# Attention and FFN on one core: quad 5 loaded and rearranged one step sooner, quad 8 later

## The chip, the cores and the metric

The kernel runs on one core of a Trainium2 chip. A core has five engines that run side by side, each through its own list of instructions in order: TensorE (PE in the profile, with its weight loads as PEld), VectorE (DVE), ScalarE (ACT), GpSimd (POOL) and SyncE (SP). They wait for one another by semaphores. Transfers are issued by POOL, SP and ACT and carried out by 16 DMA engines, which all of them share. The metric is the device time of one launch in microseconds (us), and less is better. Before the change the median of 11 runs is 386.49 us (386.11 to 389.3).

## The reference

Attention without a softmax (relu squared instead), then a feed-forward layer with a leaky activation whose slope is learnt:

```python
def _attn_ref(q, k, v):                     # 8 batches, 12 heads, 448 tokens, 64 wide
    scores = scale * np.matmul(q, k.transpose(0, 1, 3, 2))
    attn = np.maximum(scores, 0.0) ** 2 / S
    return np.matmul(attn, v)

def _moe_ref(x, w_in, w_out, alpha):        # 3584 tokens, 768 wide, 2048 inside
    h = x @ w_in
    g = np.maximum(h, 0.0) + alpha * np.minimum(h, 0.0)
    return g @ w_out
```

The heads of a token, side by side, are the row `x`. All inputs and the output are float32 in memory.

## The kernel before, in words

The four heads of one batch that are worked on together are called a quad here; 8 batches make 24 quads, n = 0 to 23. All work in SBUF is in bf16.

*Loads.* POOL issues the loads of q, k and v (`load_qk`, L100; `load_v`, L107) and of the weights (`load_w_in`, L117; `load_w_out`, L122), and they turn float32 into bf16 on the way. w_out is held as two tiles: `w_out[0]` with the first 256 columns, `w_out[1]` with the other 512; a call loads 4 of 16 row groups at a time. The raw q and k have three buffers each, so quad n + 3 can only be loaded when quad n has been read. A further rule is in the program that the compiler makes of it: each load of POOL waits for the landing of the eighth before it.

*Turning.* Scores need q and k with the head's width on the partitions. The first five quads are transposed by PE (`turn_pe`, L156, copied out at L159). From quad 5 on `turn_dma` does it: two DVE copies put the rows into the order that is wanted (tile `perm`, L164, two buffers), and SP issues one transposing DMA (L166) into the tile `T` (four buffers). SP also issues nearly all output DMAs (L274), in program order with the transposes. `landed` (L376) is a copy of one element of quad 5's `T` by POOL: it does nothing but hold POOL's later loads until that transpose has landed.

*Attention.* A quad has seven chunks of keys. For a chunk, `score_mm` (L178) makes the scores in a pair of PSUM banks, `relu` takes them out on ACT (L187) or DVE (L189), and `square` (L195 on ACT, L197 on DVE) squares them. Chunks whose square is still to come stand in the list `late`; `sq(k, eng)` squares the first k of them, and each FFN1 step squares one (L252). `attnv(n)` (L207) multiplies a quad's squares by v and writes its part of xT (L217, L218).

*FFN.* `f1(b, ff)` makes one of 16 steps of FFN1 for batch b: 6 matmuls (L241), a negated relu on ACT (L249), and a combination on DVE (L250) into gT. `f2(sb, c, h)` makes 128 tokens of FFN2 for two batches, 256 or 512 columns (h = 0 or 1), with 16 matmuls (L266), a copy to SBUF on ACT (L268) and two output DMAs.

*Order.* Nothing is scheduled by a planner: the order of the calls in the source is the order on each engine. After the first three quads, FFN1 of batch 0 is mixed with the scores of quads 3 and 4, then come the first three FFN2 groups of 256 columns, the rest of quad 4, quad 5, FFN1 of batch 1 (during which quads 7 and 8 are rearranged), and FFN2 of batches 0 and 1 mixed with quads 6 to 8. From there the pattern repeats. `prepare(n)` is `turn_dma(n)` followed by the loads of quad n + 2. The score chunks from quad 6 on are taken in order by `some(k)`, so quad 8's first chunk is the 15th; `run(some(3))` after `f2(0, 3, 1)` takes it.

Of the kernel before, what the change touches and what calls it, by code (L numbers as in the profile page):

```python
# [20 lines left out]
def kernel(  # L21
# [48 lines left out]
    def take(lo, n):  # L70
        clock[0] += 1
        for i in range(lo, lo + n):
            taken[i] = clock[0]
# [12 lines left out]
    def take_bank():  # L86
        i = min(range(8), key=lambda i: (taken[i], i))
        take(i, 1)
        return psum[:, i]
# [4 lines left out]
    def load_qk(n, names="qk"):  # L94
        b, g = divmod(n, NG)
        for name in names:
            src = q if name == "q" else k
            t = raw_pool.tile([128, 2, NJ, D], BF16, tag=name, name=f"{name}raw")
            flat = src[b].rearrange("(m two) (pp j) d -> (two pp) m (j d)", two=2, j=NJ)
            nc.gpsimd.dma_start(out=t.rearrange("p m j d -> p m (j d)"), in_=flat[:, 2 * g:2 * g + 2])  # L100
            raw[(n, name)] = t

    def load_v(n):
        b, g = divmod(n, NG)
        t = v_pool.tile([128, 2, NJ, D], BF16, tag="v", name="vraw")
        flat = v[b].rearrange("(m two) (pp j) d -> (two pp) m (j d)", two=2, j=NJ)
        nc.gpsimd.dma_start(out=t.rearrange("p m j d -> p m (j d)"), in_=flat[:, 2 * g:2 * g + 2])  # L107
        vraw[n] = t
# [11 lines left out]
    def load_w_out(h, lo=0, hi=KF, step=4):  # L120
        for lo in range(lo, hi, step):
            nc.gpsimd.dma_start(out=w_out_sb[h][:, lo:lo + step], in_=w_out_v[:, lo:lo + step, COLS[h][0]:COLS[h][1]])  # L122
# [38 lines left out]
    def turn_dma(n):  # L161
        p = perm_pool.tile([128, 2, NJ, 2, D], BF16, tag="perm", name="perm")
        for i, name in enumerate("qk"):
            nc.vector.tensor_copy(p[:, i], raw.pop((n, name)).rearrange("p s j d -> p j s d"))  # L164
        t = T_pool.tile([128, 2, NJ, 128], BF16, tag="T", name="T")
        nc.sync.dma_start_transpose(out=t.rearrange("p a j c -> p (a j) c"),  # L166
                                    in_=p.rearrange("p a j s d -> p (a j s d)"))
        T[n] = t
# [23 lines left out]
    def square(n, j, rl, eng="D"):  # L192
        a = at_pool.tile([128, 2, S], BF16, tag="at", name="at")
        if eng == "A":
            nc.scalar.activation(a, rl, ACTF.Square)  # L195
        else:
            nc.vector.tensor_tensor(a, rl, rl, ALU.mult)  # L197
        att[(n, j)] = a
# [21 lines left out]
    late = []  # L220

    def sc(chunks):

        for n, j, eng in chunks:
            late.append((n, j, relu(score_mm(n, j), eng)))

    def sq(k=99, eng="D"):
        for g in late[:k]:
            square(*g, eng)
        del late[:k]  # L230

    def run(chunks):
        sc(chunks)
        sq()
# [4 lines left out]
    def f1_mm(ps, b, ff, ks):  # L239
        for km in ks:  # L240
            nc.tensor.matmul(ps, w_in_sb[:, km // 2, km % 2, bass.ts(ff, 128)],  # L241
                             xT[b][:, km // 2, km % 2, :],
                             start=(km == 0), stop=(km == KM - 1))

    def f1_out(ps, b, ff):
        if b // 2 not in gT:
            gT[b // 2] = g_pool.tile([128, KF, 2 * S], BF16, tag="g", name="gT")
        neg = neg_pool.tile([128, S], F32, tag="neg", name="neg")
        nc.scalar.activation(neg, ps, ACTF.Relu, scale=-1.0)  # L249
        nc.vector.scalar_tensor_tensor(gT[b // 2][:, ff, (b % 2) * S:(b % 2) * S + S],  # L250
                                       neg, beta_sb[:, ff:ff + 1], ps, ALU.mult, ALU.add)
        sq(1)  # L252

    def f1(b, ff):
        ps = take_bank()[:, :S]
        f1_mm(ps, b, ff, range(KM))
        f1_out(ps, b, ff)

    def f2(sb, c, h, parts=None):

        first_col, width = COLS[h][0], COLS[h][1] - COLS[h][0]
        o = o_pool.tile([128, d_model - CUT], F32, tag="o", name="osb")
        for lo, hi in parts or ((0, width),):
            ps = take_bank()[:, :hi - lo]
            for ff in range(KF):
                nc.tensor.matmul(ps, gT[sb][:, ff, bass.ts(c, 128)], w_out_sb[h][:, ff, lo:hi],  # L266
                                 start=(ff == 0), stop=(ff == KF - 1))
            nc.scalar.copy(o[:, lo:hi], ps)  # L268
            for u in range(2):
                blk = 2 * c + u  # L270
                b, j = 2 * sb + blk // NJ, blk % NJ
                rows = out[b * S:(b + 1) * S].rearrange("(pp j) d -> j pp d", j=NJ)
                eng = nc.scalar if u and parts else nc.sync
                eng.dma_start(out=rows[j][:, first_col + lo:first_col + hi], in_=o[64 * u:64 * u + 64, lo:hi])  # L274
# [4 lines left out]
    def ch(n, lo, hi, p=pat):  # L279
        return [(n, j, p[j]) for j in range(lo, hi)]  # L280
# [22 lines left out]
    sq(1)  # L303
    sc([(1, 4, "D"), (1, 5, "A"), (1, 6, "A")])
    sq(2)
    load_w_out(0, 0, 8)
    load_qk(5)
    load_v(3)
    load_w_out(0, 8)
    early = {}  # L310
# [31 lines left out]
    def f1s(b, lo, hi):  # L342
        for ff in range(lo, hi):
            f1(b, ff)

    def load(n):
        if n < NQ:
            load_qk(n)
            load_v(n)
# [13 lines left out]
    f1_mm(ps, 0, 9, range(KM))  # L363
    turn_pe(4, (("q", 0, NJ, "A"), ("k", 0, NJ, "D")))
    f1_out(ps, 0, 9)
    f1s(0, 10, 12)
    sc(ch(3, 6, 7) + ch(4, 0, 2, "AA"))
    turn_dma(5)
    f1s(0, 12, 13)
    kept = late[:]  # L370
    del late[:]
    f1s(0, 13, 16)
    late += kept
    load_qk(6)
    load_qk(7, "q")
    nc.gpsimd.tensor_copy(landed, T[5][:1, 0, 0, :1])  # L376
    load_qk(7, "k")
    load_qk(8)
    load_w_out(1)
    load_v(6)  # L380
    f2(0, 0, 0)
    sq()
# [23 lines left out]
    def some(k):  # L406
        lo = at_c[0]
        at_c[0] = min(lo + k, len(chunks))
        return [(n, j, e) for (n, j), e in zip(chunks[lo:at_c[0]], "ADA")]
# [18 lines left out]
    for ff in range(KF):  # L428
        if ff < 5:
            f1_mm(psum[:, early[ff], :S], 1, ff, range(4, KM))  # L430
            f1_out(psum[:, early[ff], :S], 1, ff)
            take(early[ff], 1)
        else:
            f1(1, ff)
        if ff in (1, 10):
            turn_dma(7 + ff // 9)
        if ff == 1:
            load(10)
    f2(0, 3, 0)
    run(some(3))  # L440
    f2(0, 0, 1)
    run(some(3))
    f2(0, 1, 1)
    f2(0, 2, 1)
# [71 lines left out]
```

## Time and profile before

| | |
|---|---|
| median of 11 runs | 386.49 us |
| profiled execution, its own time | 387.24 us |
| its span (first to last instruction) | 385.3 us |
| PE busy | 375.0 us, 97% |
| DVE, ACT, POOL busy | 266.1, 206.8, 67.8 us |
| DMA moved | 43.42 MB, mean 113 GB/s |

The page puts the span into 40 equal slices, with the busy share of each engine in tenths. A chain of work that ended last is followed back from the last instruction, from each instruction to what released it. A wait names the instruction that waited, what ended the wait, the total in us, how often and the longest. In views in order of time a row has its start and its length in us, the engine, the source line, the operation, what it writes and reads, and in brackets the engine's idle time before it and what ended that. A DMA's row is the time in which it was issued; its landing is told apart.

### The profile page before, as it was taken

The page shows a single profiled execution, that of the slowest core. Times are in us where ns is not written, and L with a number is a line of the kernel's source. Part 1 is how long each engine was busy: PE and PEld are TensorE (multiplying, and loading weights), DVE is VectorE, ACT ScalarE, POOL GpSimd, SP SyncE. Part 2 cuts the span into 40 slices and gives each one's busy share as a digit, 9 for nine tenths or more (in the row PEclk, how much of TensorE's full clock was granted, in tenths as well). Part 3 has the DMA queues.
Part 4 walks back from the last instruction along what each step waited for, and adds up shares of the span by engine and source line. Part 5 has one row for each costly group of instructions (what it writes and reads, how often), then busy time and mean ns, then how long its engine had stood idle before and what let it go on. Part 6 is the DMA issues. An engine that isn't in the chain of part 4 may idle for free.

```text
span 385.3 us, 7838 instructions
## 1 busy us (share of the span) xinstructions
PE 375.0 (97%) x3178; PEld 205.9 (53%) x3200; DVE 266.1 (69%) x422; ACT 206.8 (54%) x331; POOL 67.8 (18%) x102
## 2 busy tenths in 40 slices
PE   7799989999999999999999999999999999999996
PEld 6444554545554455555465455544556445645554
DVE  3987987765768888689655897779855788526300
ACT  4977686545364664555445555637544375434321
POOL 8557236222202202022100222020000000000000
PEclk9999999999999999999999999999999999999999
DMA  9999999999892675698292871946036300120023
GB/s 158 190 202 202 201 126 216 180 194 228 160 192 50 112 126 90 115 142 114 53 161 59 145 122 43 173 67 124 20 79 94 77 0 16 43 68 2 14 68 84
DMA packets 73284, 43.42 MB, mean 113 GB/s; under 512 B 40352, under 2 KB 69792, under 8 KB 73248
## 3 DMA queue, kind: packets, MB, share of 16 engines
q0 software_dynamic: 26864, 22.45, 39.4%
q1 hardware_dynamic: 45952, 20.07, 27.0%
q8 instruction: 25, 0.41, 0.4%
q10 hardware_dynamic: 432, 0.39, 0.3%
q14 instruction: 11, 0.09, 0.1%
HBM read 45.62 MB, written 11.01 MB: 147 GB/s over the span
## 4 chain that ended last, share of the span: by engine, by line
PE 91%; DMA 4%; DVE 3%; issue 0%; ACT 0%; ACTq 0%
PE psum L241 38%; PE psum L266 37%; PE psum L178 9%; PE psum L207 8%; DMA T<-perm 3%; DVE at L197 2%; DMA qfirst<-in_q_dram 1%; PE psum L156 1%; DVE T L159 1%; DVE rl L189 1%; ACT osb L268 0%; ACTq L274 0%; DVE qraw L140 0%
## 5 line engine op out<-in xcount | busy, mean ns | idle before, releaser
L266 PE MATMUL psum<-w_out,gT 128*128 128x256 bf16 (+3 forms) x890 | 149.8, 322 | 1.2
L241 PE MATMUL psum<-xT,w_in_sb 128*128 128x448 bf16 x768 | 149.9, 353 | 0.0
L266 PEld LDWEIGHTS <-gT 128*128 128x128 bf16 x912 | 86.7, 98 | 64.2 <-issue 8.2
L241 PEld LDWEIGHTS <-w_in_sb 128*128 128x128 bf16 x768 | 73.6, 98 | 73.0 <-issue 5.7
L250 DVE SCALAR_TENSOR_TENSOR gT<-neg,beta_sb,psum 128x448 bf16<-128x448 f32 x128 | 83.5, 677 | 35.6 <-ACT neg L249 35.5
L249 ACT ACTIVATE neg<-psum 128x448 f32<-128x448 f32 x128 | 69.2, 546 | 61.2 <-PE psum L241 59.4
L187 ACT ACTIVATE rl<-psum 128x896 bf16<-128x896 f32 x113 | 97.9, 931 | 2.6 <-PE psum L178 2.6
L197 DVE TENSOR_TENSOR at<-rl 128x896 bf16<-128x896 bf16 x164 | 91.6, 616 | 0.0
L189 DVE TENSOR_SCALAR rl<-psum 128x896 bf16<-128x896 f32 x55 | 59.7, 1086 | 40.3 <-PE psum L178 40.2
L268 ACT COPY osb<-psum 128x256 f32<-128x256 f32 (+3 forms) x57 | 26.9, 473 | 104.4 <-PE psum L266 98.7
L178 PE MATMUL psum<-T 64*64 64x448 bf16 x672 | 44.7, 356 | 3.8 <-DVE T L159 1.4
L100 POOL DMA_DIRECT2D qraw<-in_q_dram x23 | 16.6, 720 | 156.6 <-DVE perm L164 149.7
L207 PE MATMUL psum<-at,vraw 64*64 64x448 bf16 x672 | 36.6, 350 | 0.3 <-DVE at L197 0.2
L178 PEld LDWEIGHTS <-T 64*64 64x64 bf16 x672 | 16.5, 105 | 22.5 <-issue 12.5
L207 PEld LDWEIGHTS <-vraw 64*64 64x64 bf16 x672 | 20.9, 106 | 12.6 <-issue 2.3
L218 DVE TENSOR_SCALAR xT<-psum 128x448 bf16<-128x448 f32 x23 | 14.4, 624 | 14.5 <-PE psum L207 10.9
L107 POOL DMA_DIRECT2D vraw<-in_v_dram x24 | 17.5, 728 | 7.3 <-DMA w_out<-in_moe_w_out_dram 4.3
L100 POOL DMA_DIRECT2D kraw<-in_k_dram x23 | 16.6, 722 | 6.1 <-DMA w_out<-in_moe_w_out_dram 3.4
L217 ACT ACTIVATE xT<-psum 128x448 bf16<-128x448 f32 x23 | 12.6, 549 | 2.6 <-PE psum L207 2.6
L164 DVE COPY perm<-qraw 128x896 bf16<-128x896 bf16 x19 | 11.6, 611 | 0.0
L164 DVE COPY perm<-kraw 128x896 bf16<-128x896 bf16 x19 | 11.5, 608 | 0.0
L117 POOL DMA_DIRECT2D w_in_sb<-in_moe_w_in_dram x16 | 10.1, 633 | 7.4 <-DMA kraw<-in_k_dram 2.6
(25 smaller groups left out, 41.7 us busy)
## 6 DMA issues: line engine op xcount, KB each, us to landing
out_dram<-osb SPq DMA_DIRECT2D x54, 128.0 KB, 2.4
vraw<-in_v_dram POOLq DMA_DIRECT2D x24, 224.0 KB, 8.0
qraw<-in_q_dram POOLq DMA_DIRECT2D x23, 224.0 KB, 5.4
kraw<-in_k_dram POOLq DMA_DIRECT2D x23, 224.0 KB, 7.1
out_dram<-osb SPq DMA_DIRECT2D x56, 64.0 KB, 2.2
w_in_sb<-in_moe_w_in_dram POOLq DMA_DIRECT2D x16, 192.0 KB, 8.5
w_out<-in_moe_w_out_dram POOLq DMA_DIRECT2D x4, 512.0 KB, 11.6
w_out<-in_moe_w_out_dram POOLq DMA_DIRECT2D x4, 256.0 KB, 8.9
```

Of the source, the lines that this page charges most:

```text
L100: nc.gpsimd.dma_start(out=t.rearrange("p m j d -> p m (j d)"), in_=flat[:, 2 * g:2 * g + 2])
L164: nc.vector.tensor_copy(p[:, i], raw.pop((n, name)).rearrange("p s j d -> p j s d"))
L178: nc.tensor.matmul(ps[64 * c:64 * c + 64, r, :S], t[64 * r:64 * r + 64, 1, j, 64 * c:64 * c + 64], t[64 * r:64 * r + 64, 0, :, 64 * c:64 * ...
L187: nc.scalar.activation(rl, ps[:, :, :S], ACTF.Relu)
L189: nc.vector.tensor_scalar(rl, ps[:, :, :S], 0.0, None, ALU.max)
L197: nc.vector.tensor_tensor(a, rl, rl, ALU.mult)
L207: nc.tensor.matmul(ps[64 * s:64 * s + 64, r, :S], vv[64 * r:64 * r + 64, s, j, :], a[64 * r:64 * r + 64, s], start=(j == 0), stop=(j == NJ ...
L241: nc.tensor.matmul(ps, w_in_sb[:, km // 2, km % 2, bass.ts(ff, 128)], xT[b][:, km // 2, km % 2, :], start=(km == 0), stop=(km == KM - 1))
L249: nc.scalar.activation(neg, ps, ACTF.Relu, scale=-1.0)
L250: nc.vector.scalar_tensor_tensor(gT[b // 2][:, ff, (b % 2) * S:(b % 2) * S + S], neg, beta_sb[:, ff:ff + 1], ps, ALU.mult, ALU.add)
L266: nc.tensor.matmul(ps, gT[sb][:, ff, bass.ts(c, 128)], w_out_sb[h][:, ff, lo:hi], start=(ff == 0), stop=(ff == KF - 1))
L268: nc.scalar.copy(o[:, lo:hi], ps)
```

## The change

Five calls move. Rows 4 to 7 of 16 of w_out's first 256 columns are loaded after quad 5's q and k instead of before them. Quad 5 is rearranged right after FFN1's step 11 of batch 0, ahead of three score chunks and of a square that stood before it; a square of quad 3 that is left over by that goes to ACT after step 15. Both q and k of quad 7 are loaded after `landed` (before, q stood ahead of it). w_out's 512 columns are loaded ahead of quad 8's q and k. And quad 8 is rearranged, and its transpose issued, after FFN2's first group of 512 columns, instead of after step 10 of batch 1's FFN1; what is computed is the same.

```diff
     sq(2)
-    load_w_out(0, 0, 8)
+    load_w_out(0, 0, 4)
     load_qk(5)
+    load_w_out(0, 4, 8)
     load_v(3)
     load_w_out(0, 8)
@@
     f1_out(ps, 0, 9)
-    f1s(0, 10, 12)
+    f1s(0, 10, 11)
+    kept = late[:]
+    del late[:]
+    f1s(0, 11, 12)
+    turn_dma(5)
+    late += kept
     sc(ch(3, 6, 7) + ch(4, 0, 2, "AA"))
-    turn_dma(5)
     f1s(0, 12, 13)
     kept = late[:]
     del late[:]
     f1s(0, 13, 16)
     late += kept
+    sq(1, "A")
     load_qk(6)
-    load_qk(7, "q")
     nc.gpsimd.tensor_copy(landed, T[5][:1, 0, 0, :1])
-    load_qk(7, "k")
+    load_qk(7)
+    load_w_out(1)
     load_qk(8)
-    load_w_out(1)
     load_v(6)
@@
-        if ff in (1, 10):
-            turn_dma(7 + ff // 9)
         if ff == 1:
+            turn_dma(7)
             load(10)
     f2(0, 3, 0)
     run(some(3))
     f2(0, 0, 1)
+    turn_dma(8)
     run(some(3))
```

## The prediction

> **What bounds the kernel now.** I read the page first (busy shares, the 40 slices), then the chain that ended last, then the waits of TensorE (PE), then the order of time on each engine around the one wait found, and last the landing times of the single transposing DMAs. "Quad n" is a group of four heads; T5 to T9 are the transposed q and k of quads 5 to 9.
>
> ```profile
> PE 375.0 (97%) x3178; PEld 205.9 (53%) x3200; DVE 266.1 (69%) x422; ACT 206.8 (54%) x331; POOL 67.8 (18%) x102
> PE   7799989999999999999999999999999999999996
> ```
>
> PE is busy 375.0 of 385.3 us, so it sets the time; only time in which PE idles can be won, and only new PE idling can be lost. The first two and the last slice are the start and the tail, which the change doesn't touch. PE's waits between 40 and 110 us are one line:
>
> ```profile
> PE psum L178 <- DMA T<-perm: 1.0, 1, 1.0
> ```
>
> and the chain shows where:
>
> ```profile
> 41.02 2.71 PE psum L241 x14
> 43.74 10.62 DMA T<-perm
> 54.36 0.04 issue
> 54.41 0.76 PE psum L178 x12
> ```
>
> This is T5: issued at 43.74, landed 54.36, while PE had nothing left to do from 53.42 (0.99 us idle before its score matmuls at 54.41). VectorE (DVE) and GpSimd (POOL) around it, in order of time (start, duration):
>
> ```profile
> 41.38 0.67 DVE L250 SCALAR_TENSOR_TENSOR gT<-neg,beta_sb,psum 128x448 bf16<-128x448 f32 x1
> 41.97 0.62 DVE L197 TENSOR_TENSOR at<-rl 128x896 bf16<-128x896 bf16 x1
> 42.51 0.61 DVE L164 COPY perm<-qraw 128x896 bf16<-128x896 bf16 x1
> 43.04 0.61 DVE L164 COPY perm<-kraw 128x896 bf16<-128x896 bf16 x1
> ...
> 42.09 0.71 POOL L100 DMA_DIRECT2D qraw<-in_q_dram  x1 [0.41 <-issue]
> 54.42 0.18 POOL L376 COPY landed<-T 1x1 bf16<-1x1 bf16 x1 [11.61 <-DMA T<-perm]
> 54.90 0.71 POOL L100 DMA_DIRECT2D kraw<-in_k_dram  x1 [0.30 <-PE psum L178]
> ```
>
> The rearrangement starts as soon as DVE reaches it (no idle before it), and POOL is held 11.61 us at `landed`, with quad 7's q already queued ahead of it. The DMA engines are full on both sides of that stretch (columns: stretch, its length, busy time of PE, PEld, DVE, ACT, POOL, clock, DMA share, GB/s):
>
> ```profile
> 20.00:50.00 30.00, 30.00 (x303) 15.55 (x296) 25.33 (x43) 22.56 (x37) 14.52 (x21) 1.00 1.29 201
> 50.00:58.00 8.00, 7.01 (x87) 4.79 (x85) 6.70 (x11) 6.29 (x10) 3.13 (x6) 1.00 1.08 110
> 58.00:92.00 34.00, 33.90 (x229) 16.70 (x230) 22.66 (x38) 17.45 (x29) 12.88 (x18) 1.00 1.25 197
> ```
>
> Two later rows price the other half of the change, quad 8: ScalarE's (ACT's) copy of FFN2's first 512-column result, which SyncE's (SP's) output DMA waits for, and the first scores that read T8:
>
> ```profile
> 83.33 0.58 ACT L268 COPY osb<-psum 128x512 f32<-128x512 f32 x1 [2.20 <-PE psum L266]
> ...
> 99.43 0.76 PE L178 MATMUL psum<-T 64*64 64x448 bf16 x12
> ```
>
> [...] The packet records agree: with T8 in flight both queues move some 178 packets a microsecond[...]; and the outputs issued behind T8 (from 82.97) move only after it has landed at 92.94. [...] The landings agree: 5.7 us from issue for T6, which met a nearly empty POOL queue, 10.6 for T5 and 16.4 for T7, which met a full one. [...] Here T5's bar on SP is 5.33 us and its landing 10.62 after issue, so I count landings.
>
> **The change, part by part.** In the compiled order PE's instructions are unchanged in kind and order. So the change acts only on when PE's inputs land and when PSUM is freed.
>
> 1. *Rows of quad 5 ahead of rows 4 to 7 (of 16) of w_out's first 256 columns.* One 256 KB load moves behind two of 224 KB. In order of landing that load took 39.30 − 37.96 = 1.34 us, so q5 and k5 land 1.3 us sooner (40.43 to 39.1, 41.56 to 40.2). By itself worth nothing in before's order (DVE arrives at 42.51); with part 2, DVE arrives at 41.97 and k5 would have been there with 0.4 us to spare; now 1.8. The moved w_out rows land by 41.6, read from 45.9 at the earliest (FFN2 starts at 45.52): hidden, 4 us of cover.
>
> 2. *Rearrangement of quad 5 one FFN1 step sooner.* The 0.54 us square that stood ahead of it goes behind, so the two copies start at 41.97, and T5's issue goes from 43.74 to 43.2: 0.54 us gained. One square (quad 3, j = 6) goes from DVE to ACT after the 16th FFN1 step. Price 0.93 to 0.95 (ACT's squares at 50.86); ACT idles 1.20 us there, from 46.26 to its FFN2 copy at 47.46: hidden, 0.25 us of cover left; beyond it, it would delay that copy only, whose PSUM bank is not needed until later. DVE does one square less. Cost 0.
>
> 3. *Quad 7's q behind `landed`, POOL's order after it.* The load of q7 leaves the queue that T5 shares: its landing (53.37) came 1.53 us after k6's (51.84); at 201 GB/s its 224 KB is 1.1 us of the engines. So T5 has 0.54 us of head start and 1.1 to 1.5 us less traffic. Bounds on T5's landing: no better than now if something else held it (54.36), and 54.36 − 0.54 − 1.5 = 52.3 at best; I take the gains as partly overlapping, 52.8. PE needs it by 53.37 (its own 53.42 less the 0.05 from landing to matmul): a gain of 0.99 suffices. The wait goes, **0.99 us**. What is late next: T5's scores come 0.99 us sooner, at 53.42; ACT is free at 53.83, before its first relu would be due (53.85); DVE finishes rearranging quad 6 at 53.80 and its relu, at 55.10 now, would start at 54.1. Nothing is late by 0.1 us. The rearrangement of quad 6 needs k6, landed 51.84, at 52.66.
>
> 4. *w_out's 512 columns ahead of quad 8's rows.* After `landed` (sooner by 1.5) POOL issues q7, k7, four w_out loads, q8, k8. The last w_out load lands now at 75.40; with one 224 KB load less in front net and an earlier start it lands near 72; FFN2 reads it from 79.67. It wasn't waited for: 0. Quad 8's rows go from 63.36 to about 75; the rearrangement needs them at 81.3: hidden by 6 us.
>
> 5. *Rearrangement of quad 8 behind FFN2's first 512-column group.* The two copies (1.14 us on DVE) go from 72.84 to right after the squares that end at 82.30, less the 0.99 us: 81.3 to 82.45. DVE's next instruction, a relu at 83.85 now, is due at 82.86: hidden by 0.4. On SP, T8 comes behind the two outputs of that group: ACT's copy ends 83.92 − 0.99 = 82.9, two issues at some 0.58 each, T8 issued at 84.1 instead of 74.04. It must land by 99.43 − 0.99 = 98.4: **14.3 us** are there. T7 showed its first packets 3.7 us after issue (66.31 to 70.0); T8's transfer is 1,792 packets of 256 bytes, 10.1 us at 178 a microsecond: landing at 97.9 with POOL's queue full to the end. POOL's loads of quad 11 now wait for this rearrangement (from 82.5, not 80.27), those of quad 12 for quad 9's; when T8's packets begin (87.8) I count about six loads left, 6 × 1.53 = 9.2 us (the spacing of landings in that stretch), so the last of T8 moves alone: near 97. Hidden, by 0.5 to 1.5 us, where now it has 6.5 (landed 92.94). T9 follows at about 102, needed by 106.5; T7 no longer has T8 behind it and is needed at 90. The outputs behind T8 are six or so tiles of 10 in their pool: no wait.
>
> Sum: −0.99 (wait for T5) + 0 + 0 + 0 + 0. Profiled execution: 387.24 (385.3 span, 1.9 around it) to 386.25. It stands 0.75 above the median; if all of that were a longer wait for T5, the usual run would have only 0.24 of it to lose. So the gain in the median lies in 0.24 to 0.99; I take 0.9, as launch or tracing can as well make the 0.75: **385.6**.
>
> **Rivals.**
> *T5 is no earlier.* Its slowest packets at 51 to 53 us aren't q7's but its own. For it: POOL's queue has almost run out of packets by 51, and T5 still takes 3 us. Against: T6 took 5.7 us in all when alone. Then only the 0.54 counts at best: 386.0 to 386.5.
>
> *T8 becomes the wait* (the other side). Place: scores of quad 8's first chunks, 98.4. Price: each us that T8 lands after 98.4 is PE idle. At T7's measured 16.4 us from issue it lands at 100.5, 2.1 us late: 386.49 − 0.9 + 2.1 = 387.7; at T8's own 18.9 us of before, 103.0, 4.6 late: 390.2. It is slower by over 0.3% from 16.4 us on. For it: the two transposes issued in that full stretch took just these. Against: 18.9 includes waiting for T7 until 82.7; T7 shared with w_out's larger packets (148 a microsecond) and with a slice near 73 us in which all packets were slow; and the POOL queue runs dry sooner now.
>
> *More is won.* Where the usual run waits longer for T5 than the profiled one: 1.6 us gained, 384.9. Only the spread of the eleven runs (386.11 to 389.3) speaks for it.
>
> **How the numbers follow.** 0.3% (1.16 us), about what a measurement of this kernel can tell from no change, puts the bounds at 385.33 and 387.65. Wait gone and T8 in time: 0.55, own range 385.2 to 386.3, about a third of it beyond the bound, since the whole wait is 0.26%. T5 no earlier: 0.12, no change. T8 late: 0.22, most of it over 387.65. More won: 0.11. Faster 0.19 + 0.11 = 0.30; slower 0.20; the rest 0.50. The range from 384.9 leaves half the last case below, and to 387.8 most of the T8 case above.
>
> **What would show it.** Right: T5 issued near 43.2 and landed before 53.4, no wait of PE for T in 40 to 110, POOL's `landed` near 53, T8 issued near 84 and landed by 98, PE's first scores of quad 5 at 53.4, the span about 384.3. Wrong: a wait of the score matmuls (L178) for T at 53 or at 98, ACT's added square delaying the FFN2 copy past 47.5, DVE's copies waiting for q6, k6 or q8, k8.

## The result and the profile after

The changed kernel is slower. Its median is 393.11 us over 12 runs (387.69 to 398.04), against 386.23 us over 44 runs (385.61 to 389.3) of the kernel before. The ratio is 1.0106, with a 95% interval of 1.0083 to 1.0129; it leaves out runs more than 1.5% above the fastest of the same kernel, so it stands below the quotient of the medians. The scatter is new: the kernel before keeps most of its runs within 0.7 us.

The profiled execution of the changed kernel took 387.69 us, with a span of 385.9: it is the fastest of its runs. Its busy shares hardly differ from before:

```profile
PE 375.1 (97%) x3178; PEld 206.1 (53%) x3200; DVE 265.8 (69%) x421; ACT 207.8 (54%) x332; POOL 68.0 (18%) x102
PE   7799999999899999999999999999999999999996
```

There is one 8 in PE's row, in the 11th slice (96 to 106 us). The waits of PE between 40 and 110 us (total, times, longest):

```profile
PE psum L178 <- DMA T<-perm: 1.6, 1, 1.6
```

The line reads as before, with 1.6 in place of 1.0, but it is another transpose. The chain that ended last tells which (start, length):

```profile
49.81 3.60 PE psum L266 x32
53.41 0.69 PE psum L178 x12
...
82.92 1.17 PE psum L266 x5
84.09 15.95 DMA T<-perm
100.04 0.04 issue
100.08 0.76 PE psum L178 x12
```

At 53.41 quad 5's scores follow FFN2 without a gap: the wait for T5 is gone. At 100.08 quad 8's scores wait for T8, issued at 84.09 and landed at 100.04. PE was ready 1.65 us before that. The start of the change, on VectorE, GpSimd and ScalarE in order of time:

```profile
41.37 0.67 DVE L250 SCALAR_TENSOR_TENSOR gT<-neg,beta_sb,psum 128x448 bf16<-128x448 f32 x1
41.96 0.61 DVE L164 COPY perm<-qraw 128x896 bf16<-128x896 bf16 x1
42.49 0.61 DVE L164 COPY perm<-kraw 128x896 bf16<-128x896 bf16 x1
```

```profile
51.85 0.39 POOL L381 COPY landed<-T 1x1 bf16<-1x1 bf16 x1 [10.59 <-DMA T<-perm]
52.34 0.72 POOL L100 DMA_DIRECT2D qraw<-in_q_dram  x1
```

```profile
46.15 0.94 ACT L195 ACTIVATE at<-rl 128x896 bf16<-128x896 bf16 x1
47.45 0.37 ACT L268 COPY osb<-psum 128x256 f32<-128x256 f32 x1 [0.36 <-PE psum L266]
```

The square is gone from ahead of the two copies, they start at 41.96, and POOL is released at 51.85 instead of 54.42. The first load behind `landed` goes out at 52.34; before, at 54.90. SP's own rows show what that does to the next transposes (start and time of issue, not of transfer). The one of T6 before:

```profile
53.87 1.52 SPq L166 DMA_TRANSPOSE T<-perm  x1
```

And after:

```profile
53.87 7.57 SPq L166 DMA_TRANSPOSE T<-perm  x1
...
65.24 10.50 SPq L166 DMA_TRANSPOSE T<-perm  x1
...
84.09 5.42 SPq L166 DMA_TRANSPOSE T<-perm  x1
```

The first is T6, at the same 53.87 as before. It took SP 1.52 us to issue then, and takes 7.57 now. Its landing came 5.7 us after issue before, and comes 18.4 us after it now. The busy times by stretch (length, PE, PEld, DVE, ACT, POOL, clock, DMA share, GB/s):

```profile
50.00:58.00 8.00, 8.00 (x97) 5.14 (x95) 7.75 (x13) 6.40 (x11) 6.05 (x9) 1.00 0.76 112
84.00:100.00 16.00, 14.33 (x118) 7.09 (x118) 10.61 (x17) 7.24 (x11) 3.79 (x6) 1.00 1.26 202
```

PE wins back its 0.99 us in the first stretch, and loses 1.65 in the last. The span says the same: 385.3 − 0.99 + 1.65 = 385.96, measured 385.9. So one wait was traded for a larger one. But that is only the fastest run, and the median is 5 us above it.

The landings, from issue to landing in us, of the traces that matter below. "2nd" is a later trace of the changed kernel, of a run of 392.15 us; the other columns are experiments. The last row has the transfer that PE waited for, and how long.

| | before | changed | 2nd | T6 held | T8 early | T6, T8 held |
|---|---|---|---|---|---|---|
| T5 | 43.74 to 54.36 | 43.19 to 51.80 | 42.79 to 51.96 | 42.94 to 51.72 | 43.20 to 51.83 | 43.34 to 52.62 |
| T6 | 53.87 to 59.60 | 53.87 to 72.26 | 53.47 to 68.72 | 53.61 to 58.20 | 53.87 to 70.17 | 54.02 to 58.50 |
| T7 | 66.31 to 82.67 | 65.24 to 85.60 | 64.84 to 82.86 | 65.09 to 81.82 | 65.25 to 83.96 | 65.47 to 82.75 |
| T8 | 74.04 to 92.94 | 84.09 to 100.04 | 84.61 to 101.62 | 83.83 to 100.04 | 73.98 to 94.22 | 84.24 to 97.13 |
| T9 | 93.60 to 102.29 | 92.25 to 104.75 | 93.79 to 110.97 | 92.58 to 107.02 | 96.03 to 107.57 | 92.56 to 100.00 |
| PE waits | T5, 0.99 | T8, 1.65 | T8, 3.63 | T8, 1.91 | w_out, 1.08 | none |

### The profile page after: what moved, and what is told of

It is laid out like the page before. It is cut to its first block, busy times and chain, and to the rows that moved or that the text cites. A ratio compares the mean times of both kernels' runs of the same rounds, so it can differ in the third digit from the quotient of the medians.

```text
span 385.9 us, 7838 instructions
## 1 busy us (share of the span) xinstructions
PE 375.1 (97%) x3178; PEld 206.1 (53%) x3200; DVE 265.8 (69%) x421; ACT 207.8 (54%) x332; POOL 68.0 (18%) x102
## 4 chain that ended last, share of the span: by engine, by line
PE 90%; DMA 5%; DVE 3%; issue 0%; ACT 0%; ACTq 0%
PE psum L241 38%; PE psum L266 35%; PE psum L178 8%; PE psum L207 8%; DMA T<-perm 4%; DVE at L197 2%; DMA qfirst<-in_q_dram 1%; PE psum L156 1%; DVE T L159 1%; DVE rl L189 1%; ACT osb L268 0%; ACTq L274 0%; DVE qraw L140 0%
```

## The experiments

Two theories stood at first. A: T8's later issue alone makes T8 late. B: the late issue is harmless, and T8 is late because `landed` comes sooner, the loads then get ahead of T6, and the whole train of transposes is pushed back. All ratios are to runs of the kernel before on the same chip. Each diff is against the kernel that its expectation names first.

### The changed kernel again

> The changed kernel once more, for a second trace and a second set of times. If the wait for T8 (landed 100.04, 1.6 us late in the first trace) is what costs, a run at 391 us or above must show a longer wait of the score matmuls for T8, some 1.6 us plus the excess over 387.7 (5 us at 391), or further waits for T6 or T7; all other waits of PE stay as they are. If something else costs (matmuls that run slower by themselves), the wait stays near 1.6 us and the excess is spread over the span.

388.19 to 392.37 us in four runs, median 390.09, ratio 1.0103 (1.0062 to 1.0145). The trace fell on the fastest of them again (388.19, span 386.2): PE waits 1.96 us for T8, landed at 100.36, and for nothing else after 20 us. A run above 391 came into a trace only later (below). It confirms the first of the two expectations in kind, a longer wait for T8 and no other, but not in size: the wait was 3.63 us where some 6 were forecast. The rest was matmuls that ran slower (twelve score matmuls in 1.33 us in place of 0.76), which is a part of the second expectation.

### T8 issued late, and nothing else changed

```diff
-        if ff in (1, 10):
-            turn_dma(7 + ff // 9)
         if ff == 1:
+            turn_dma(7)
             load(10)
     f2(0, 3, 0)
     run(some(3))
     f2(0, 0, 1)
+    turn_dma(8)
```

> The kernel before, with only quad 8's rearrangement and transpose moved behind FFN2's first 512-column group. Theory A (the late issue alone makes T8 late, since any transpose issued into a full POOL queue takes about 16 us): T8 issued near 85.1, landed near 101, needed at 99.4, so PE waits 1.5 us or more on top of the 1.0 for T5: 387.7 us or above, with runs as scattered as the changed kernel's. Theory B (the late issue is harmless, T8 was late because T6 and T7 were pushed back by loads that begin sooner after landed): T6 lands near 60 as before, T7 near 81, T8 14 us after issue or sooner: 386.2, no change.

386.95 us in the median of 14 runs, ratio 1.0025 (1.0017 to 1.0034). In the trace T8 is issued at 83.75 and lands at 98.72, after 15.0 us; PE's scores wait 0.67 us, until 98.76. (The list of waits puts this down to a copy of ACT that ended at the same 98.72. But in the kernel before, these scores start at 99.43, ahead of that copy at 99.54, so they don't need it.) T6 lands at 60.81. So A holds in kind: the late issue does cost, with T6 landing only 1.2 us later than before. But it costs 0.25%, less than A's 387.7, and the runs stay within 386.3 to 388.0: it isn't the whole loss. This trace also shows T5 landing at 52.96 in the order of before, with no wait for it: the wait of 0.99 us isn't in every run of the kernel before.

### Quad 5 sooner, T8 as early as before

```diff
     load_qk(7)
-    load_w_out(1)
     load_qk(8)
+    load_w_out(1)
@@
-        if ff == 1:
-            turn_dma(7)
+        if ff in (1, 10):
+            turn_dma(7 + ff // 9)
+        if ff == 1:
             load(10)
@@
-    turn_dma(8)
```

> The changed kernel, with quad 8's rearrangement back after step 10 of batch 1's FFN1 and quad 8's rows ahead of w_out's 512 columns again; quad 5 sooner as in the change. Theory A: the wait for T5 stays gone and T8 is in time: 385.3 us (1.0 below before), T6 landing near 72 as in the changed kernel, T7 near 84, T8 near 95, needed at 98.4. Theory B: the transposes are still pushed back from T6 on, PE waits for T7 or T8 by 1 us or more: 387 us or above.

389.32 us in the median of 4 runs, ratio 1.0098 (1.0059 to 1.0137). T8 is in time (94.22), so A's forecast of 385.3 is wrong: the first half of the change costs about as much alone as the whole change. B's time is right, but not its wait. T6 takes 16.3 us and T7 18.7, which both theories expected, and what PE waits for in the trace isn't a transpose:

```profile
PE psum L266 <- DMA w_out<-in_moe_w_out_dram: 1.1, 1, 1.1
```

It is the last load of w_out's 512 columns, which lands at 82.41 (75.40 before, 75.46 in the changed kernel, where quad 8's rows are behind it). So with loads released early, T6 moves beside everything that comes behind `landed`, and the loads are late as well as the transposes. The traced run is the fastest of the four (span 385.4). What the two at 390 and 391 us waited for wasn't traced.

### POOL held for T6 instead of T5

```diff
-    nc.gpsimd.tensor_copy(landed, T[5][:1, 0, 0, :1])
-    load_qk(7)
-    load_w_out(1)
-    load_qk(8)
-    load_v(6)
     f2(0, 0, 0)
@@
     turn_dma(6)
+    nc.gpsimd.tensor_copy(landed, T[6][:1, 0, 0, :1])
+    load_qk(7)
+    load_w_out(1)
+    load_qk(8)
+    load_v(6)
     load_qk(9)
```

> The changed kernel, with POOL held until T6 has landed in place of T5, so that no load runs beside T6. T6 lands 6 us after issue (60) in place of 18. Theory A: T8 is still issued at 84.1 into a full queue, lands near 100, PE waits 1.5 us or more: 387.5 us or above. Theory B: T7 and T8 are back to 14 us or less, no wait: 385.3 us.

388.02 us in the median of 5 runs, ratio 1.005 (1.003 to 1.0069). T6 lands 4.6 us after issue, and T8 is still late: 16.2 us, landing at 100.04. That is A's forecast. The loss is about half as large (the intervals, 0.30 to 0.69% and 0.62 to 1.45%, just meet). T8's landing doesn't explain that, since it is the same as in the first trace of the changed kernel; but none of these five runs is above 389.6. And the trace shows something that neither theory had. The wait is 1.91 us, yet the span is 387.6, 3.4 above the 384.2 that most runs of the kernel before have. The clock column, the third from the end, tells where the rest went:

```profile
90.00:100.00 10.00, 8.18 (x88) 4.34 (x80) 7.99 (x12) 5.88 (x9) 1.43 (x2) 1.00 1.30 182
100.00:105.00 5.00, 4.92 (x24) 1.88 (x25) 3.75 (x6) 1.73 (x2) 0.77 (x2) 0.66 1.24 232
105.00:110.00 5.00, 5.00 (x70) 3.23 (x67) 1.09 (x1) 2.71 (x5) 1.37 (x2) 1.00 1.24 239
```

Between 100 and 105 us, behind the wait, PE's granted clock was 0.66 in the mean: 0.34 × 5 = 1.7 us lost. The chain agrees: from the start of these scores to the next ones the same matmuls take 7.76 us (100.08 to 107.84), where the changed kernel's first trace has 6.07 (100.08 to 106.15). 384.2 + 1.9 + 1.7 = 387.8, measured 387.6. How the 5 us split isn't shown; half clock for some 3.4 us, as the filler's expectation below has it, is an estimate from these 1.7 us. The last section sets five waits beside the clock measured behind them.

### Both halves undone, quad 5 still sooner

The previous kernel with quad 8 as before: its rows ahead of w_out's 512 columns, and `turn_dma(8)` after step 10 of FFN1.

> Quad 5 loaded and rearranged sooner as in the change; POOL held until T6 has landed; quad 8's rows ahead of w_out's 512 columns and its rearrangement after step 10 of FFN1, as before. It joins the two halves undone so far. Theory C (two independent losses: T8 issued late, worth about 0.5%, and loads that start ahead of T6 because landed comes sooner, worth about 1% with T8 early): both are gone, T6 lands near 59, PE waits for no T, 385.9 to 386.3 us, no change to before. Rival (the sooner rearrangement of quad 5 or the load order at the start cost by themselves): still 387 us or above.

386.72 us in the median of 20 runs, ratio 1.0014 (1.0007 to 1.002). It differs from the "T8 early" kernel only in what POOL is held for, and the loss goes from 0.98% to 0.14%: letting the loads in beside T6 is what cost there. It held up the loads too: w_out's last one lands at 80.74, 1.7 us sooner than in that kernel, though all of them start 6 us later. The small rest is more than the nothing that Theory C forecast. In the trace PE waits 0.18 us for T9 (landed 106.48); that the later loads now meet the later transposes is a likely reason, and isn't shown.

### Only quad 5 sooner

```diff
-    load_w_out(0, 0, 8)
+    load_w_out(0, 0, 4)
     load_qk(5)
+    load_w_out(0, 4, 8)
@@
-    f1s(0, 10, 12)
-    sc(ch(3, 6, 7) + ch(4, 0, 2, "AA"))
+    f1s(0, 10, 11)
+    kept = late[:]
+    del late[:]
+    f1s(0, 11, 12)
     turn_dma(5)
+    late += kept
+    sc(ch(3, 6, 7) + ch(4, 0, 2, "AA"))
@@
+    sq(1, "A")
```

> The kernel before, with only the first two parts: quad 5's rows ahead of four row groups of w_out, rearrangement one FFN1 step sooner, one square on ACT; quad 7's q stays ahead of landed, everything later as before. T5 lands near 52.5. Theory C: if T6 lands near 60 (loads of POOL start near 53, T6 is issued near 53.5), 386.0 us, no gain, since the usual run of the kernel before (span 384.2) has no wait for T5 left; if the sooner landed puts loads ahead of T6 (T6 near 70), 388 us or above. Rival (the first prediction's gain is there): 385.2 us.

386.15 us in the median of 12 runs, ratio 0.9999 (0.9989 to 1.0008): no difference. T5 lands at 53.12, for which PE waits 0.16 us, and T6 at 61.48. So these two parts neither win nor cost. There was nothing to win: the 18 runs of the kernel before beside the first four experiments have spans of 383.9 to 384.6, and its profiled execution less its 0.99 us of wait is 385.3 − 0.99 = 384.3. The usual run doesn't wait for T5.

### PE kept busy while T8 is late

```diff
     f2(0, 3, 1)
+    fill = take_bank()
+    for _ in range(16):
+        nc.tensor.matmul(fill, ident, w_out_sb[1][:, 0, :], start=True, stop=True)
     run(some(3))
     f2(0, 4, 1)
```

> The changed kernel with 16 matmuls that nobody reads (128x512, about 0.21 us each, 3.4 us) ahead of quad 8's first scores, so that PE stays busy while T8 is late. If the loss is the wait alone: runs rise by 3.4 less the wait that they cover, 391 to 392 us in the median. If a wait of 2 us and more also halves PE's clock for some 3.4 us afterwards (1.7 us lost each time, as in the trace of the kernel with POOL held for T6): those drops at 100 us are gone, the clock of most runs is back at 0.999 or 1.0, and the median stays at or under 390 us in spite of the added work. Clock below 0.996 in most runs would mean that the waits lie elsewhere.

389.55 us in the median of 4 runs (389.03 to 389.64), ratio 1.0083 (1.0068 to 1.0098), clock 0.999 or 1.0 in all. In the trace T8 lands at 100.32, and PE waits for nothing after 40 us. 3.4 us more of work makes the kernel no slower than it was, and nearly all the scatter is gone. The spans, 387.2 to 387.8, are the floor of 384.2 and the 3.4 us added: in these runs nothing else is lost. It was then run beside the changed kernel on another chip:

> The changed kernel beside the three others on one chip, for a comparison with the kernel that keeps PE busy. As before: 389 to 394 us, runs scattered over several us, clock below 0.997 in about half of them.

> The changed kernel with 3.4 us of matmuls that nobody reads ahead of quad 8's first scores. If T8's wait and the clock drop after it are the whole loss: 389.5 us, all runs within 1 us, clock 0.998 or more: as fast as or faster than the changed kernel's median on the same chip, though PE does 3.4 us more. If the loss also lies elsewhere: as scattered as the changed kernel, 3 us above it.

The changed kernel: 387.51 to 394.19 us in 10 runs, median 390.26, ratio 1.0084 (1.0046 to 1.0122). This time a run of 392.15 us was traced. PE in order of time, and the stretches behind it:

```profile
94.41 3.63 PE L266 MATMUL psum<-w_out,gT 128*128 128x512 bf16 x15
101.66 1.33 PE L178 MATMUL psum<-T 64*64 64x448 bf16 x12 [3.63 <-DMA T<-perm]
```

```profile
95.00:101.60 6.60, 3.04 (x14) 1.18 (x12) 3.47 (x6) 1.07 (x2) 0.71 (x1) 0.91 1.31 186
101.60:105.00 3.40, 3.34 (x17) 1.10 (x18) 2.33 (x4) 1.73 (x2) 0.00 (x0) 0.50 1.30 197
105.00:110.00 5.00, 5.00 (x26) 2.70 (x25) 1.42 (x3) 0.58 (x1) 2.15 (x3) 0.77 1.27 149
```

T8 took 17.0 us, PE waited 3.63, and behind the wait the clock was half for 3.4 us and 0.77 in the 5 us after: (0.50 × 3.4) + (0.23 × 5) = 2.9 us lost. This run is 0.4 us ahead of the first trace from T5's issue on (42.79 against 43.19), so its floor is 384.3 − 0.4 = 383.9. 383.9 + 3.6 + 2.9 = 390.4, measured 390.2. The twelve score matmuls alone show it: 1.33 us in place of 0.76. So the wait for T8 and the clock after it are the whole excess of this run, to 0.2 us.

The kernel with the filler: 390.26 us in the median of 5 runs, ratio 1.0095 (1.0082 to 1.0109), not told apart from the changed kernel's. Four runs lie between 389.07 and 390.68, at a clock of 0.999 or 1.0; the fifth took 395.36 and is the one traced. That misses the "all within 1 us". Its wait for T8 is 0.16 us, covered as meant; what it waits for is the next transpose, T9, which lands at 114.07 behind the late T8:

```profile
PE psum L178 <- DMA T<-perm: 4.1, 2, 3.9
```

So the lateness can travel on to T9. In the changed kernel's three traces it didn't.

### POOL held until T8 has landed

```diff
     f2(0, 0, 1)
     turn_dma(8)
+    nc.gpsimd.tensor_copy(landed, T[8][:1, 0, 0, :1])
     run(some(3))
```

> The changed kernel with POOL held until T8 has landed ahead of the loads of quads 11 and 12, so that T8 meets only the loads queued before (up to quad 10's v, landing near 92). If the loads beside it make T8 slow: T8 lands near 97, in time (98.4), and T6 stays slow (71): 386 to 387 us where only T8 costs, more where T6 or w_out cause waits too. If T8's 16 us are its own (start and transfer): still near 100, wait 1.6 us, 388 us or above.

> The changed kernel with POOL held until T8 has landed, again. Seven of its 20 runs stood at 387.8 to 390.4, the others at 385.8 to 386.7. If T6's crowded transfer is behind these (T6 or w_out's last load in time in one run and 2.5 us late in another), they come back here and not in the kernel that is held for T6 as well.

386.22 us in the median of 20 runs, ratio 1.002 (1.0003 to 1.0038), and 386.16 us in 22 runs, ratio 1.0015 (1.0 to 1.003). T8, issued at 84.2 and 84.1, lands at 91.96 and 95.99, in place of 100.04: with the loads of quads 11 and 12 out of its way, the same transpose at the same time takes 7.8 and 11.9 us instead of 16. So T8's 16 us aren't its own. T6 still takes 17.5 and 20.1 us. In both sets about a third of the runs stand at 387.1 to 390.4; neither trace fell on one of them.

### POOL held for T6 and for T8

The kernel held for T6, with that line for T8 added.

> The changed kernel with POOL held for T6 in place of T5, and once more until T8 has landed. T6 lands near 58, T8 within 8 to 10 us of its issue at 84 although it is issued as late as in the change. If the loads beside the transposes are the whole cause: 385.9 to 386.4 us, no run above 387.5. If the runs at 388.6 of the kernel that is held for T8 alone come back, their cause isn't T6's company.

386.19 us in the median of 13 runs (385.64 to 386.28), ratio 1.0 (0.9992 to 1.0008). T6 takes 4.5 us, T8 12.9 (landed 97.13, PE reads it at 98.52), T9 7.4, and PE waits for nothing between 40 and 110 us. This is the changed kernel with T8 issued as late as in the change, and the loss is gone, with all runs within 0.65 us. On this chip the changed kernel loses 0.84%, with POOL held for T8 alone 0.15%, and with both holds nothing: loads beside the two transposes are the cause. The runs above 387 of the kernel held for T8 alone don't come back either, which speaks for T6's crowded transfer as their cause; their own wait wasn't seen, so that stays open.

None of these kernels is clearly faster than the one before, and the traces say why: without a wait after 20 us the span is 384, and the usual run of the kernel before is there already.

## Why the prediction was wrong

It forecast 385.6 us, in a range from 384.9 to 387.8. The profiled run of 387.69 lies just inside it, the median of 393.11 far outside.

*Part 1, quad 5's rows sooner: right.* q5 and k5 land at 38.88 and 40.01 (forecast 39.1 and 40.2), the moved w_out rows at 41.35 (41.6), and nothing waits.

*Part 2, rearrangement sooner, one square on ACT: right.* T5 is issued at 43.19 (43.2). ACT squares from 46.15 for 0.94 us and copies FFN2's result at 47.45, where it did before.

*Part 3, T5's wait: the mechanism right, the gain wrong.* T5 lands at 51.80 (52.8) and the scores start at 53.41. But the 0.99 us was a wait of one execution. The prediction saw that this execution stood 0.75 us above the median, gave the gain as 0.24 to 0.99, and took 0.9. Over all 44 runs the median is 386.23, 1.01 us below this execution: the whole wait. So the usual run had nothing to give, and the experiment with parts 1 and 2 alone says the same, 0.0 within 0.1%.

*Part 3, "what is late next": incomplete, and this is the first step that failed.* It looked at ACT and DVE and left out SP's next transpose. T6 isn't moved by the change, since it waits for quad 6's rearrangement at 53.8. The loads behind `landed` are. Before, they went out from 54.90, 1.0 us after T6's issue; now from 52.34, 1.5 us ahead of it. T6 went from 5.7 to 18.4 us. Over all the traces T6 by and large takes the longer, the sooner that first load goes out: 4.3 to 4.6 us where it goes out 5 us after T6's issue, 7.4 and 8.0 where it goes out 0.0 and 0.2 after it, 12.4 where it is 0.6 ahead, 15.3 at 1.0, and 15.8 to 20.1 at 1.4 to 1.6. In the one pair of kernels that differ in just this, the loss is 0.98% against 0.14%.

*Part 4, w_out and quad 8's rows: right that nothing waits, the times wrong.* w_out's last load lands at 75.46 (forecast 72) and quad 8's k at 78.61 (75), while T6 moved beside them until it landed at 72.26. The reserve for the rearrangement at 81.3 shrank from 6 us to 2.7.

*Part 5, T8: the decisive step.* Its issue at 84.09 (84.1) and its deadline at 98.4 came out right. The transfer was counted at 13.8 us with a full queue, and somewhat less with "about six loads left", so that the last part would move alone. Measured are 15.95, 16.3 and 17.0 us. The packet records of the first trace say which terms were too small, even for a full queue: 4.2 us to the first packet instead of 3.7, 11.3 us of packets (159 a microsecond) instead of 10.1 (178), and 0.5 us from the last packet to the landing, which the sum left out. (T7's first packet in the kernel before was at 70.21, 3.9 us after issue, not 3.7.) And the queue didn't run dry: from 87.8 on seven loads landed before T8 did, and two more were under way (quad 12's k at 101.11, its v at 103.12). T7's 16.4 us, which the rival used, had all of this in it. "Hidden, by 0.5 to 1.5 us" was the term that was mis-sized: it was late by 1.65 to 3.63. The trials with POOL held for T8 show that the loads beside it make it so.

*The rivals.* "T8 becomes the wait" is what happened, at the place named, and its figure for a transfer of 16.4 us, 387.7, fits the profiled run. It priced a late microsecond at one microsecond, as the prediction's first step did ("only new PE idling can be lost"). That holds for waits of 1.65 and 1.96 us, whose runs have a mean clock of 1.0 and 0.999; a wait of 1.91 us in another kernel cost 3.6, and one of 3.63 cost 6.5. The clock is only part of why the median lies past the range, though. The two runs at the median (393.07 and 393.14, spans 391.1 and 391.2, 6.9 and 7.0 above the floor) have a mean clock of 0.991 on record, which is some 3.5 us of the span at most. So they waited some 3.4 us or more as well, and that alone would make about 389.5. "T5 is no earlier" and "More is won" are excluded by T5's landing and by the experiment on quad 5.

*A reading of the packets.* Between 83 and 92 us of the kernel before, with T8 in flight, each of the two queues moved 1,589 packets, 176.6 a microsecond. The equal rate is all that the records show of how the two share the engines: they don't tell which engine moved which packet. And the outputs behind T8 began to move at 92.08, when T8's last packets were on their way, not after its landing at 92.94.

*What stays open.* Which waits make the longest runs, which were never traced: a wait for T8 with the clock after it explains 6.5 us above the floor, and the runs of 395 and 398 us have 9 and 12. A run of 392.14 us has an excess of 6.0 us at full clock. The waits of 3.63 and 3.9 us that were traced had a lowered clock behind them, so several shorter waits are likelier here than one of 6 us; this is an estimate from those two traces. T9, as in the filler's trace, may be part of it.

## What to carry to other kernels

A hold that lets one queue go when a transfer has landed can also shelter the transfer after it, as `landed` did T6 (5.7 us to landing before, 18.4 after the change); before making the first one land sooner, ask what the released queue will meet, and hold for the last transfer that needs the shelter. When a transpose is issued later into a busy stretch, take as its duration, from issue to landing, that of one in the same trace that met an equally full queue (here T7's 16.4 us, measured 15.95 to 17.0), and count the queue beside it from the new landings, not the old ones. A wait seen in a single profiled execution is worth checking against the spans of the other runs: what they don't have can't be won.

## What the runs showed of the hardware

*Transposes.* A transpose of one quad (1,792 packets of 256 bytes) landed 4.3 to 5.7 us after issue where it was T6 and met a nearly empty queue of POOL, and 15.0 (T8, issued late and nothing else changed) to 20.4 us after it (T7 of the changed kernel) when the queue stayed full. For T6 the start of POOL's loads at 52.34 in place of 54.90 went with 18.4 us in place of 5.7. T8, issued at 84.1 to 84.2, took 15.95 us with POOL's loads beside it and 7.8, 11.9 and 12.9 us with POOL held.

*PE's clock.* Five waits, and the granted clock that was measured with them:

| trace | wait for, us | clock |
|---|---|---|
| changed | T8, 1.65 | 1.00 from 84 to 106 us |
| changed again | T8, 1.96 | 0.999 in the mean of the run |
| T6 held | T8, 1.91 | 1.00 from 90 to 100 us, 0.66 from 100 to 105, 1.00 from 105 to 110 |
| 2nd | T8, 3.63 | 0.91 from 95 to 101.6 us, 0.50 to 105, 0.77 to 110, 1.00 to 115 |
| filler, later trace | T9, 3.9 | 1.00 from 110 to 114 us, 0.65 to 118, 0.92 to 122, 1.00 to 126 |

The wait of 1.91 us had a lowered clock behind it, worth 1.7 us, and left its run with a mean clock of 0.996. The wait of 1.96 us had no such loss: its run has 0.999. So a wait of about 2 us cost 2.0 us in one trace and 3.6 in another. What makes the difference isn't shown, nor how long a wait must be for the clock to fall. That is one source of the scatter.
